# Dilated values loaded one unit sooner and the plain queries behind them, in a banded attention and top-1 expert kernel

## The chip, the core and the metric

The kernel runs on one core of a Trainium2 chip. The metric is the device time of one execution in microseconds (us), as the median of several runs. Five engines work beside each other: TensorE (PE, matrix products and transposes; PEld is its loading of weights), VectorE (DVE), ScalarE (ACT), GpSimd (POOL) and SyncE (SP), which here does little else than issue DMAs. Each engine works off its own instructions in order.

## The reference

Eight batches of eight heads attend over 576 positions of 64 values each. Heads 0 to 3 are plain: a query sees the 32 positions up to itself. Heads 4 to 7 are dilated: a query sees every fourth position back to 128. The attended rows (4608 tokens of 512 values) then go through a mixture of eight experts, of which each token takes the one with the highest gate.

```python
scores = scale * np.matmul(q, k.transpose(0, 1, 3, 2))
rel = pos[:, None] - pos[None, :]
mask_plain = (rel >= 0) & (rel < window)
mask_dil = (rel >= 0) & (rel < window * dilation) & (rel % dilation == 0)
masks = np.stack([mask_plain if h < H // 2 else mask_dil for h in range(H)], axis=0)
scores = np.where(masks[None, :, :, :], scores, -1000000000.0)
...
return np.matmul(attn, v).astype(np.float32)
```

```python
logits = x @ w_gate + modality_bias[modality_id]
e_idx = np.argmax(logits, axis=1)
...
    h = np.maximum(x[mask] @ w1[e], 0.0)
    out[mask] = gate_w[mask, None] * (h @ w2[e])
```

## The kernel before

The attention comes first and the experts after it. The attention is cut into 72 units, nine for each batch `b`, counted by `m` from 0 to 8 within the batch and by `t` over all. A unit takes two blocks of 64 queries with all four heads of a kind. Units 0 to 3 are plain (`kd == 0`), unit 4 takes the last block of each kind, and units 5 to 8 are dilated (`kd == 1`). For the dilated heads the positions are sorted by their rest modulo 4, so that the band is as narrow as that of the plain ones.

A loop over `t` writes the order of work out by hand: under the manual schedule PE, DVE, ACT and SP keep the order in which the loop emits instructions. One pass `t` emits the scores of unit `t` (line 340, and the adding of the mask on DVE at line 343), the exponential of unit `t-1`, the products with the values of unit `t-3` (`attend`, line 365), the gate logits of unit `t-5`, the transposes of the probabilities of unit `t-2`, the store of unit `t-4`, then the copies `shift_v` (ACT, line 137), and then the transposes of queries and keys that a coming unit needs (`qk_chunks`: PE at line 306, ACT copies at 309 and 311). `step()` and `advance()` put in work of the experts and of the routing.

The loads for a batch are sixteen DMAs of 144 KB for queries and keys of both kinds, and 1152 KB of values, half of it for each kind:

- `load_one` (line 116) loads queries or keys of one kind, in four DMAs, one for each head, into one of four buffers `st`. The transposes of `qk_chunks` read them. There are six pieces for a kind, keys and queries in turn; for the plain kind the first two pieces need heads 0 and 1 only, the next two heads 2 and 3, and the last two all four. Two pieces are done in a pass: the plain ones of batch `b+1` in passes `m` = 4, 5 and 6 of batch `b`, the dilated ones in passes 8, 0 and 1.
- `load_v` loads the values into one of three buffers `vw`: the plain ones in one DMA (line 127), the dilated ones in twelve small ones (line 131), because each block of 64 sorted positions may touch two residues. `shift_v` then copies the last 32 rows of each block to the top of the next, one head in pass 4, one in pass 5 and two in pass 6 for the dilated kind. One head's copy reads eight of the nine blocks, which the first eleven of the twelve DMAs fill.

The dilated values of batch `b+1` go to the buffer that held the plain values of batch `b`. Its last reader is `attend` of unit 4, which pass 7 emits.

All these loads are issued by SP in the order in which the loop emits them. For one batch before the change that is: keys of the plain kind in pass 6 (for two batches ahead), queries of the plain kind in pass 7, the first six pieces of the dilated values in pass 8, the other six at the start of pass 0, dilated keys in pass 1, dilated queries in pass 2 and plain values in pass 3.

After the eighth batch's units the experts run in slots of 256 tokens. The first slots are filled from the routing of the first five batches: POOL gathers their rows into `xr`, SP writes these to `x_slot` and reads them back as `xg` in passes of the last two batches.

Of the kernel before, what the change touches and what calls it, by code (L numbers as in the profile page):

```python
# [22 lines left out]
B, H, S, D = 8, 8, 576, 64  # L23
# [28 lines left out]
def _csegs(c0, c1):  # L52

    segs, c = [], c0
    while c < c1:
        r = c // CL
        n = min(c1, (r + 1) * CL) - c
        segs.append((c - c0, r, c - r * CL, n))
        c += n
    return segs  # L60
# [4 lines left out]
def kernel(  # L65
# [43 lines left out]
    def vw(b, kd):  # L109
        return vws[(2 * b + kd) % 3]  # L110

    def load_one(b, kd, src, queue=nc.sync):

        t = ald.tile([PQ, SI, 4, D], F32, name="st")
        for h in range(4):
            queue.dma_start(out=t[:, :, h], in_=src[b, 4 * kd + h].rearrange("(p s) d -> p s d", s=SI))
        return t

    def load_qk(b, kd, queue=nc.sync):
        kn = load_one(b, kd, k)  # L120
        return load_one(b, kd, q, queue), kn

    def load_v(b, kd, part=slice(None)):

        t = vw(b, kd)
        if kd == 0:
            nc.sync.dma_start(out=t[WIN:KW, :, :, 0:D], in_=v[b, 0:4].rearrange("h (i p) d -> p h i d", p=TQ))
        else:
            vv = v[b, 4:8].rearrange("h (j r) d -> r j h d", r=NCLS)
            for i, o, r, j, n in [(i, *seg) for i in range(NTILE) for seg in _csegs(TQ * i, TQ * (i + 1))][part]:  # L130
                nc.sync.dma_start(out=t[WIN + o:WIN + o + n, :, i, 0:D], in_=vv[r, j:j + n])
        return t

    def shift_v(b, kd, h):

        t = vw(b, kd)
        nc.scalar.copy(out=t[0:WIN, h, 1:NTILE].rearrange("p i d -> p (i d)"), in_=t[TQ:KW, h, 0:NTILE - 1].rearrange("p i d -> p (i d)"))

    state = {('qk', 0, 0): load_qk(0, 0, nc.scalar)}
# [142 lines left out]
    def qk_chunks(kd, qn, kn):  # L282


        def chunk(n, is_q):
            src = qn if is_q else kn
            pt = psum['o'].tile([P, 512], F32, name="po") if is_q and psum['many'] else ps_t.tile([P, 512], F32, name="pt")
            flat = qT[kd] if is_q else kT[kd][:, :, WIN:]
            inp = pt[:, 0:4 * PQ]
            if kd == 0:  # L290

                gs, s0, ns = ((n,), 0, 4) if n < 2 else ((0, 1), 4, 2)
                inp = inp.rearrange("c (g p i) -> c g p i", g=len(gs), i=ns)
                jobs = [(inp[:, x, :, i], s0 + i, g) for x, g in enumerate(gs) for i in range(ns)]
                parts = [(flat[:, gs[0]:gs[-1] + 1].rearrange("c g (p s) -> c g p s", s=SI)[:, :, :, s0:s0 + ns], inp)]
            else:
                inp = inp.rearrange("c (g i p) -> c g i p", g=2, p=PQ)
                jobs = [(inp[:, g, i], 2 * n + i, g) for g in range(2) for i in range(2)]

                parts = []  # L300
                for e in range(2):
                    o = 6 * e + 2 * n
                    dst = flat.rearrange("c g (r j t) -> c g r t j", r=NCLS, t=3)[:, :, o % 4:o % 4 + 2, o // 4]
                    parts.append((dst, inp.rearrange("c g i (j e) -> c g i e j", e=2)[:, :, :, e]))
            for to, i, g in jobs:
                nc.tensor.transpose(out=to, in_=src[:, i, 2 * g:2 * g + 2].rearrange("p a d -> p (a d)"), identity=ident[:PQ, :PQ])
            for dst, src in parts:
                if is_q:
                    nc.scalar.mul(dst, src, 1.0 / 8.0)
                else:  # L310
                    nc.scalar.copy(out=dst, in_=src)
        return [(lambda n=n, is_q=is_q: chunk(n, is_q)) for n in range(SI // 2) for is_q in (False, True)]
# [368 lines left out]
    NU = len(order)  # L681
# [233 lines left out]
    units, pieces, dilated = [], [], []  # L915
# [11 lines left out]
    def step(share=MOE_RATE / 6):  # L927

        nonlocal credit
        if moe:  # L930
            credit += share if state['t'] < NU else 1
            while credit >= 1:
                credit -= 1
                next(moe, None)

    def advance(some=range(-1, B)):
        for b, task in tasks:
            if b in some:
                next(task, None)

    state['routed'] = False
    for t in range(NU + LAG + 1):
        state['t'] = t
        if 'go' in state and not moe:
            octx.close()
            psum['many'] = False
            psum['y'] = ctx.enter_context(tc.tile_pool(name="ps_y", bufs=2, space=PSUM))
            psum['o'] = ctx.enter_context(tc.tile_pool(name="ps_o1", bufs=1, space=PSUM))
            moe = slots(NS, ids_of, ahead, hold)
        b, m = t // 9, t % 9  # L950
        if t == 1:
            pieces = qk_chunks(1, *state['qk', 0, 1])
        if t < NU:
            jobs = order[t][1]
            if m == 0:
                state['lT', b] = gwk.tile([2 * NE, S], F32, name="lT")
            if b + 1 < B:
                if m == 4:
                    pieces = qk_chunks(0, *state['qk', b + 1, 0])
                elif m == 8:  # L960
                    pieces = qk_chunks(1, *state['qk', b + 1, 1])
            if m == 0 and b > 0:
                load_v(b, 1, slice(6, None))
            elif m == 3:
                if b + 1 < B:
                    state['v', b + 1, 0] = load_v(b + 1, 0)
            units.append(Unit(b, m, jobs, [state['v', b, 0], state['v', b, 1]] if m >= 4 else [state['v', b, 0]], state['lT', b]))
            units[t].scores()
        step()
        if 0 <= t - 1 < NU:  # L970
            units[t - 1].exp()
        po = psum['o'].tile([P, 512], F32, name="po")
        if 0 <= t - 3 < NU:
            units[t - 3].attend(po)
        step()
        if 0 <= t - LAG < NU:
            units[t - LAG].logits(po)
        if 0 <= t - 3 < NU:
            units[t - 3].normalize()
        if 0 <= t - LAG < NU:  # L980
            units[t - LAG].gather_logits()
            if (t - LAG) % 9 == 8:
                tasks.append(((t - LAG) // 9, background((t - LAG) // 9)))
        step()
        advance()
        if 0 <= t - 2 < NU:
            units[t - 2].probsT()
        step()
        if 0 <= t - 4 < NU:
            units[t - 4].store()  # L990
            units[t - 4].keep(pool)

        for h in {0: (0,), 1: (1,), 2: (2, 3)}.get(m, ()) if 2 < t < NU else {0: (0, 1), 1: (2, 3)}.get(t, ()):
            shift_v(b, 0, h)
        for h in {4: (0,), 5: (1,), 6: (2, 3)}.get(m, ()) if t < NU else ():
            shift_v(b, 1, h)
        for i in range(2):
            step()
            if i < len(pieces):
                pieces[i]()  # L1000
        pieces = pieces[2:]
        if t < NU and b + 1 < B:

            if m == 1:
                state['k', 1] = load_one(b + 1, 1, k)
            elif m == 2:
                state['qk', b + 1, 1] = load_one(b + 1, 1, q), state['k', 1]
            elif m == 6 and b + 2 < B:
                state['k', 0] = load_one(b + 2, 0, k)
            elif m == 7 and b + 2 < B:  # L1010
                state['qk', b + 2, 0] = load_one(b + 2, 0, q), state['k', 0]
            elif m == 8:
                state['v', b + 1, 1] = load_v(b + 1, 1, slice(0, 6))
        advance([*round_of, B - 1] if moe and t < NU else range(-1, B))


# [40 lines left out]
```

## Time and profile before

| what | value |
|---|---|
| time, median of 3 runs | 711.53 us (710.65 to 712.71) |
| time of the profiled execution | 710.85 us |
| span of the profiled execution, first to last instruction | 709.1 us |
| busy share of the span: PE, DVE, ACT, POOL | 92%, 70%, 62%, 41% |
| mean granted TensorE clock | 0.959 of full speed |
| first score of the attention, last score of the attention | 14.59 us, 252.10 us |

Times in rows are microseconds from the start of the span. In a row of the timeline the first number is the start, the second the duration, then come engine, line, operation, what is written and read, and in square brackets the idle time of the engine just before the row with what ended it. "x12" says that the row merges twelve instructions that follow each other. A DMA row on SPq lasts as long as SP needs to issue; when the data lands is not in it, and shows only where somebody waits for it.

### The profile page before, as it was taken

The page shows a single profiled execution, that of the slowest core. Times are in us where ns is not written, and L with a number is a line of the kernel's source. Part 1 is how long each engine was busy: PE and PEld are TensorE (multiplying, and loading weights), DVE is VectorE, ACT ScalarE, POOL GpSimd, SP SyncE. Part 2 cuts the span into 40 slices and gives each one's busy share as a digit, 9 for nine tenths or more (in the row PEclk, how much of TensorE's full clock was granted, in tenths as well). Part 3 has the DMA queues.
Part 4 walks back from the last instruction along what each step waited for, and adds up shares of the span by engine and source line. Part 5 has one row for each costly group of instructions (what it writes and reads, how often), then busy time and mean ns, then how long its engine had stood idle before and what let it go on. Part 6 is the DMA issues. An engine that isn't in the chain of part 4 may idle for free. (4 is left out here: it accounts for less than half of the span.)

```text
span 709.1 us, 17888 instructions
## 1 busy us (share of the span) xinstructions
PE 649.3 (92%) x6286; PEld 571.1 (81%) x6286; DVE 497.4 (70%) x1212; ACT 437.9 (62%) x964; POOL 290.0 (41%) x396
## 2 busy tenths in 40 slices
PE   6799998997887899799999999999999999999991
PEld 3688787786776688689999999999999999999980
DVE  1688886886876778677766776667766677667660
ACT  3587896886766656355665565565666556655650
POOL 7345774865668553533333232233313231310110
PEclk7799999999899699999999999999999999999996
DMA  9898698697976943213433972333222346821730
GB/s 159 144 233 180 150 193 169 150 195 145 166 167 159 257 131 77 61 61 91 138 131 78 263 185 79 74 114 106 96 83 82 99 120 182 219 74 46 203 86 13
DMA packets 163233, 94.95 MB, mean 134 GB/s; under 512 B 124144, under 2 KB 143090, under 8 KB 163140
## 3 DMA queue, kind: packets, MB, share of 16 engines
q1 hardware_dynamic: 146612, 63.89, 40.3%
q0 software_dynamic: 11120, 28.64, 13.4%
q10 hardware_dynamic: 5408, 1.24, 1.0%
q8 instruction: 51, 0.84, 0.6%
q14 instruction: 42, 0.34, 0.2%
HBM read 127.52 MB, written 29.39 MB: 221 GB/s over the span
## 5 line engine op out<-in xcount | busy, mean ns | idle before, releaser
L858 PE MATMUL pt<-xh,w1l 128*128 128x256 f32 (+1 forms) x608 | 172.9, 284 | 7.7 <-DVE w1l L807 7.7
L858 PE MATMUL pt<-xl,w1h 128*128 128x256 f32 (+1 forms) x608 | 172.3, 283 | 0.0
L858 PE MATMUL pt<-xh,w1h 128*128 128x256 f32 (+1 forms) x608 | 172.2, 283 | 0.0
L864 ACT ACTIVATE hh<-pt 128x256 fp32r<-128x256 f32 (+1 forms) x152 | 57.6, 379 | 159.5 <-PE pt L858 159.4
L807 DVE TENSOR_TENSOR w2l<-w2q,w2h 128x512 fp32r<-128x512 f32 x152 | 104.9, 690 | 43.0 <-ACT w2h L806 34.7
L274 POOL DMA_INDIRECT xr<-x_dram,idt x74 | 82.5, 1115 | 120.4 <-DMA x_slot<-xr 72.2
L858 PEld LDWEIGHTS pt<-xh,w1l 128*128 128x128 f32 x608 | 116.7, 192 | 8.6 <-DVE w1l L807 8.5
L858 PEld LDWEIGHTS pt<-xh,w1h 128*128 128x128 f32 x608 | 116.5, 192 | 6.8 <-ACT w1h L806 0.2
L858 PEld LDWEIGHTS pt<-xl,w1h 128*128 128x128 f32 x608 | 116.6, 192 | 5.7
L838 PE MATMUL py<-w2h,hh 128*128 128x512 f32 x296 | 118.1, 399 | 0.0
L838 PE MATMUL py<-w2h,hl 128*128 128x512 f32 x296 | 117.1, 396 | 0.0
L838 PE MATMUL py<-w2l,hh 128*128 128x512 f32 x296 | 116.1, 392 | 0.0
L865 DVE SCALAR_TENSOR_TENSOR hl<-pt,hh 128x256 fp32r<-128x256 f32 (+1 forms) x152 | 63.3, 416 | 73.9 <-ACT hh L864 73.8
L274 POOL DMA_INDIRECT out_dram<-ys,idt x37 | 39.6, 1071 | 179.4 <-ACT ys L841 115.8
L807 DVE TENSOR_TENSOR w1l<-w1q,w1h 128x512 fp32r<-128x512 f32 x152 | 104.1, 685 | 2.7 <-ACT w1h L806 2.7
L806 ACT CAST w1h<-w1q 128x512 fp32r<-128x512 f32 x152 | 94.4, 622 | 3.3 <-DMA w1q<-in_moe_w_dram 3.3
L806 ACT CAST w2h<-w2q 128x512 fp32r<-128x512 f32 x152 | 93.1, 612 | 0.0
L274 POOL TENSOR_TENSOR sm<-sm,nmx 128x384 f32<-128x384 f32 x72 | 59.8, 830 | 61.9 <-DVE den L372 45.5
L365 PE MATMUL po<-vw,pT 96*64 96x65 f32 x1152 | 57.0, 238 | 11.3 <-ACT pT L359 6.7
L359 ACT COPY pT<-pt 96x512 f32<-96x512 f32 x72 | 41.5, 576 | 41.3 <-PE pt L356 40.2
L838 PEld LDWEIGHTS py<-w2l,hh 128*128 128x128 f32 x296 | 55.8, 189 | 13.2
L365 PEld LDWEIGHTS po<-vw,pT 96*64 96x64 f32 x1152 | 44.5, 145 | 24.6 <-ACT pT L359 11.4
(160 smaller groups left out, 1110.7 us busy)
## 6 DMA issues: line engine op xcount, KB each, us to landing
w2q<-in_moe_w_dram SPq DMA_DIRECT2D x76, 512.0 KB
w1q<-in_moe_w_dram SPq DMA_DIRECT2D x152, 256.0 KB
st<-in_k_dram SPq DMA_DIRECT2D x64, 144.0 KB
x_slot<-xr SPq DMA_DIRECT2D x18, 512.0 KB
xg<-x_slot SPq DMA_DIRECT2D x72, 128.0 KB
x_dram<-x_sb POOLq DMA_DIRECT2D x32, 256.0 KB, 3.6
st<-in_q_dram SPq DMA_DIRECT2D x56, 144.0 KB
vw<-in_v_dram SPq DMA_DIRECT2D x8, 576.0 KB
```

What stands on the lines that cost most here:

```text
L274: ins = tc.keep_in_program_order(getattr(nc.gpsimd, name)(*args, **kw))
L359: nc.scalar.copy(out=self.pT, in_=src)
L365: nc.tensor.matmul(out=pov[u * TQ:(u + 1) * TQ, h, :], lhsT=self.pT[:, h, u * TQ:(u + 1) * TQ], rhs=self.vts[kd][:, h, i, :], start=True, ...
L806: nc.scalar.copy(out=hi, in_=raw)
L807: nc.vector.tensor_tensor(out=lo, in0=raw, in1=hi.bitcast(F32), op=ALU.subtract)
L838: nc.tensor.matmul(out=py[u], lhsT=ht[:, us], rhs=wt, start=(f + n == 0), stop=(f + n == FC + 1))
L858: nc.tensor.matmul(out=ph, lhsT=wt[:, c, :], rhs=xt[:, c, 0:cols], start=(c + i == 0), stop=(c + i == KC + 1))
L864: nc.scalar.activation(out=hh, in_=ph, func=AF.Relu)
L865: nc.vector.scalar_tensor_tensor(out=hl, in0=ph, scalar=0.0, in1=hh.bitcast(F32), op0=ALU.max, op1=ALU.subtract)
```

## The change

The dilated values of the next batch are issued in passes 7 and 8 instead of 8 and 0 (the second half now at the end of pass 8 and not at the start of pass 0). The plain queries, which stood in pass 7, are issued at the end of pass 0 of the next batch, behind all twelve value pieces. In batch 0, the six pieces of dilated transposes, two in each of passes 1, 2 and 3, are done three at once in passes 2 and 3, and the copies `shift_v` of the plain values move from passes 0 and 1 to passes 1 and 2.

```diff
-        if t == 1:
+        if t == 2:
             pieces = qk_chunks(1, *state['qk', 0, 1])
...
-            if m == 0 and b > 0:
-                load_v(b, 1, slice(6, None))
-            elif m == 3:
+            if m == 3:
                 if b + 1 < B:
                     state['v', b + 1, 0] = load_v(b + 1, 0)
...
-        for h in {0: (0,), 1: (1,), 2: (2, 3)}.get(m, ()) if 2 < t < NU else {0: (0, 1), 1: (2, 3)}.get(t, ()):
+        for h in {0: (0,), 1: (1,), 2: (2, 3)}.get(m, ()) if 2 < t < NU else {1: (0, 1), 2: (2, 3)}.get(t, ()):
             shift_v(b, 0, h)
...
-        for i in range(2):
-            step()
+        at_once = 3 if t < 4 else 2
+        for i in range(at_once):
+            if i < 2:
+                step()
             if i < len(pieces):
                 pieces[i]()
-        pieces = pieces[2:]
+        pieces = pieces[at_once:]
...
-            elif m == 7 and b + 2 < B:
-                state['qk', b + 2, 0] = load_one(b + 2, 0, q), state['k', 0]
+            elif m == 7:
+                state['v', b + 1, 1] = load_v(b + 1, 1, slice(0, 6))
             elif m == 8:
-                state['v', b + 1, 1] = load_v(b + 1, 1, slice(0, 6))
+                load_v(b + 1, 1, slice(6, None))
+            elif m == 0 and b > 0:
+                state['qk', b + 1, 0] = load_one(b + 1, 0, q), state['k', 0]
```

## Rows read from the trace of the kernel before

**Rows 1.** Windows: PE, PEld, DVE, ACT, POOL busy, granted clock, DMA share.

```profile
45.00:75.00 30.00, 28.35 (x516) 24.40 (x513) 25.83 (x85) 25.23 (x63) 16.57 (x28) 1.00 0.82 182
300.00:650.00 350.00, 347.46 (x2209) 315.13 (x2210) 249.80 (x450) 208.50 (x430) 103.28 (x93) 1.00 0.41 117
```

**Rows 2.** Timeline of DVE, line 343: first unit of batches 1 to 6, last unit.

```profile
44.91 0.56 DVE L343 TENSOR_TENSOR sm<-pss,masks 128x384 f32<-128x384 f32 x1
...
71.67 0.54 DVE L343 TENSOR_TENSOR sm<-pss,masks 128x384 f32<-128x384 f32 x1
...
98.19 0.54 DVE L343 TENSOR_TENSOR sm<-pss,masks 128x384 f32<-128x384 f32 x1
...
128.14 0.54 DVE L343 TENSOR_TENSOR sm<-pss,masks 128x384 f32<-128x384 f32 x1
...
155.20 0.54 DVE L343 TENSOR_TENSOR sm<-pss,masks 128x384 f32<-128x384 f32 x1
...
187.87 0.54 DVE L343 TENSOR_TENSOR sm<-pss,masks 128x384 f32<-128x384 f32 x1
...
252.10 0.51 DVE L343 TENSOR_TENSOR sm<-pss,masks 128x384 f32<-128x384 f32 x1
```

**Rows 3.** Timeline of ACT, first copy of the dilated values in batches 3 and 5.

```profile
115.66 0.62 ACT L137 COPY vw<-vw 32x520 f32<-32x520 f32 x1 [3.91 <-DMA st<-in_k_dram]
...
173.60 0.62 ACT L137 COPY vw<-vw 32x520 f32<-32x520 f32 x1 [4.83 <-DMA st<-in_k_dram]
```

**Rows 4.** Waits up to 300 us: total, times, longest (these are batches 2, 4).

```profile
ACT vw L137 <- DMA vw<-in_v_dram: 2.4, 2, 1.5
```

**Rows 5.** Timeline of SP: loads around the dilated values of batches 1 to 7.

```profile
48.00 8.01 SPq L131 DMA_DIRECT2D vw<-in_v_dram  x12
...
70.58 2.68 SPq L116 DMA_DIRECT2D st<-in_q_dram  x4
73.36 9.58 SPq L131 DMA_DIRECT2D vw<-in_v_dram  x12
...
97.96 3.55 SPq L116 DMA_DIRECT2D st<-in_q_dram  x4
101.61 10.15 SPq L131 DMA_DIRECT2D vw<-in_v_dram  x12
...
125.42 2.98 SPq L116 DMA_DIRECT2D st<-in_q_dram  x4
128.50 9.19 SPq L131 DMA_DIRECT2D vw<-in_v_dram  x12
...
152.40 4.07 SPq L116 DMA_DIRECT2D st<-in_q_dram  x4
156.57 14.14 SPq L131 DMA_DIRECT2D vw<-in_v_dram  x12
...
183.31 2.91 SPq L116 DMA_DIRECT2D st<-in_q_dram  x4
...
206.24 0.78 SPq L127 DMA_DIRECT2D vw<-in_v_dram  x1
216.25 0.40 SPq L645 DMA_DIRECT2D x_slot<-xr  x1
```

**Rows 6.** Waits of SP over the span: total, times, longest.

```profile
SPq L131 <- DMA vw<-in_v_dram: 3.7, 3, 2.8
SPq L131 <- DMA st<-in_q_dram: 3.2, 5, 1.1
```

**Rows 7.** Timeline of PE, first transposes of plain queries in pass 4 of batch 3.

```profile
111.19 0.49 PE L306 MATMUL po<-ident,st 96*128 96x96 f32 x4
```

**Rows 8.** Timeline of PE, the same transposes in pass 4 of batch 0.

```profile
32.37 0.52 PE L306 MATMUL po<-ident,st 96*128 96x96 f32 x4 [1.38 <-DMA st<-in_q_dram]
```

**Rows 9.** Timeline of SP, the load that these transposes read.

```profile
27.52 2.60 SPq L116 DMA_DIRECT2D st<-in_q_dram  x4
```

**Rows 10.** Timeline of PE, products with the values in pass 7 of batch 5.

```profile
183.48 0.69 PE L365 MATMUL po<-vw,pT 96*64 96x65 f32 x16 [0.29 <-ACT pT L359]
```

## The prediction

> **What bounds the kernel now.** I looked first at the stages, by windows. From 300 us on, TensorE is busy 347.46 of 350 us, and in the attention 28.35 of 30 us when nothing stalls [rows 1]. The change touches loads of the attention only. The last unit of the attention starts at 252.10, and 709.1 - 252.10 = 457.0 us of experts and their routing follow [rows 2]. PE is full there, so I count what the attention gains or loses one to one at the end.
>
> Then I looked at how long a batch takes, from the first unit of one to that of the next [rows 2]: 26.8 us for batch 1 (71.67 - 44.91), 26.5 for batch 2, 29.95 for batch 3, 27.1 for batch 4, 32.7 for batch 5. Three batches agree within 0.6 us and two stick out. The waits say why. ACT's first copy of the dilated values, in pass 4, waited 3.91 us in batch 3 and 4.83 us in batch 5 [rows 3], and 2.4 us in batches 2 and 4 together, the longer one 1.5 us, so 0.9 and 1.5 us [rows 4]. The rows name keys as the releaser in the two long cases, but this copy reads no keys. The values' twelve DMAs are what it needs, and these had just been issued: SP ended them at 101.61 + 10.15 = 111.76 in batch 3, with the copy starting at 115.66, and at 156.57 + 14.14 = 170.71 in batch 5, with the copy at 173.60 [rows 3, 5].
>
> A wait does not cost its whole length. Against 26.65 us (the mean of batches 1 and 2) batch 3 lost 3.3 us for 3.91 us of waiting, batch 4 0.4 for 1.5, batch 2 nothing for 0.9. So ACT has 0.6 to 1.1 us in hand. Batch 5 lost 6.0 us; I put 4.83 - 0.6 = 4.2 us of it down to the wait, and leave 1.8 us, since the routing for the first slots runs there and nothing here says otherwise. The values' lateness costs 3.3 + 0.4 + 4.2 = 7.9 us in all. That is what the change can win.
>
> **Values sooner.** No instruction is added or removed in a batch after the first: SP issues the same DMAs in another order. The twelve value DMAs take the place of the four of the queries, so they start sooner by what the queries took: 73.36 - 70.58 = 2.8 us in batch 2, 3.65 in batch 3, 3.1 in batch 4, 4.2 in batch 5 [rows 5]. If they land sooner by as much, the waits shrink to 0, 0.26, 0 and 0.66 us. Batch 2 shows that waits of this length cost nothing. So this part gives up to 7.9 us.
>
> **Queries later.** This is the price. The queries now end where the values ended. Who needs them next is PE: the first transposes of queries in pass 4 need heads 0 and 1, so the second of the four DMAs. In batch 3 they run at 111.19, 13.0 us after the batch's first unit [rows 2, 7]; I use 13.0 us for every batch. How long after its issue does such a DMA land? In batch 0 PE waited for just this until 32.37. SP issued the four from 27.52 in 2.60 us, so the second from 28.17, and it took 4.2 us [rows 8, 9]. Heads 2 and 3 are needed a pass (3 us) later but are issued only 1.3 us later, so they land in time if heads 0 and 1 do.
>
> The bound from above takes SP's stretch of sixteen DMAs as long as before. The second query DMA then starts 1.95 us (three quarters of 2.60) before the old end of the values, and lands 4.2 us after that. Batch 3: 111.76 - 1.95 + 4.2 = 114.0 against 111.19, so PE waits 2.8 us. Batch 5: 170.71 + 2.25 = 172.96 against 155.20 + 13.0, so 4.8 us. Batch 2: 82.94 + 2.25 = 85.2 against 84.7, so 0.5. Batch 1 (58.26 against 57.9): 0.35. Batch 4 (139.9 against 141.1): none. Sum 8.45 us, with nothing in hand to swallow it, since PE is the fullest engine [rows 1].
>
> The bound from below takes 8.01 us for the twelve values, which is what they took in batch 1 [rows 5]. The second query DMA then starts 8.01 + 0.65 us after the old start of the queries and lands 4.2 us after that, so 12.9 us after it: 110.8 in batch 3 against 111.19, 165.3 in batch 5 against 168.2, 83.4 in batch 2 against 84.7. No wait at all.
>
> Which is nearer? The twelve took 10.15 us in batch 3 and 14.14 in batch 5, because SP itself waited between them for earlier DMAs to land: for queries 3.2 us in five waits and for values 3.7 us in three [rows 6]. The five behind queries go away when the queries come after; those behind values, and whatever was slow in batch 5, may come back behind the keys. Both kinds of wait weigh about the same, so I take the middle: 4.2 us of waits on PE. **Sum: 7.9 - 4.2 = 3.7 us won**, with bounds of +7.9 and -0.55.
>
> [...] The row of windows shows DMA engines at 0.82 of their time in a batch without a stall [rows 1], and SP's rows leave gaps of 0.1 us between these loads [rows 5]. [...]
>
> **SP's new wait.** The first six values may go only after PE's products of unit 4, in pass 7. In batch 5 those end at 183.48 + 0.69 = 184.17, and SP would be there at 183.31 [rows 5, 10]: SP stands for 0.9 us, with the next queries and dilated keys behind it. Both are needed some 10 us or more later, since batch 6 starts at 187.87 and its pass 4 comes 13 us after. I cost it at nothing; were that cover gone, it would be 0.9 us. In the other batches SP arrives later than that pass. In batch 6 the first six values move ahead of `x_slot`, for which SP stood idle from 207.0 to 216.25 [rows 5]. They may delay it by up to 4 us, half of 8.01, and the second six then stand behind it. The read back to `xg` follows all of these in either order, so I cost it at nothing too.
>
> **Batch 0.** Moving the dilated transposes from pass 1 to 2 lets unit 2's scores go sooner, and moving the copies of the plain values keeps ACT free. But PE waits for batch 1's queries until 32.37 anyway, and their load, issued at 27.52, has nothing moved ahead of it [rows 8, 9]. Work that gets there sooner waits longer. Bounds: a win of 1.38 us were that wait to end sooner, and a loss of about 0.9 us, a third piece's share of PE (0.49 us as in rows 7) in each of two passes. I take 0, because the DMA decides.
>
> **The number.** 710.85 - 3.7 = 707.15 us for the profiled execution. The median of the runs lies 0.7 us above it, so 707.8 us.
>
> **The rivals.** First, the wait only moves: PE waits for queries as long as ACT did for values. For it speaks the bound from above, and SP's solid rows; against it, that a part of SP's waits was for the queries ahead. Between a loss of 0.55 and a win of 2 us this gives 709.5 to 712, say 711.5. Chance 0.23.
>
> Second, it is slower: PE's waits exceed ACT's, because a query DMA behind twelve values lands later than 4.2 us after issue. If 5.2 us, each of batches 1, 2, 3 and 5 waits 1 us more than in the bound from above: 8.45 + 4 = 12.45, against 7.9 won, which gives 716 us. It decides once the landing takes 4.6 us and more with SP's stretch unshortened: 0.55 + 4 x 0.4 = 2.15 us, the 0.3% that a measurement of this kernel can tell from no change. For it speaks that the values of batch 3 needed about 4 us after the last issue [rows 3, 5]; against it, that the values are light and leave little queued before the queries. Chance 0.12.
>
> Third, the values' wait goes and none comes: 711.5 - 7.9 = 703.6 us. For it speaks the bound from below. Chance 0.15. The forecast, between 705 and 709.4 us, has 0.50. So faster has 0.65, no change 0.23, slower 0.12.
>
> The range of 702.8 to 712.5 us reaches over the third and the first; the forecast's own is 705 to 709.4.
>
> **What would show it.** After: ACT's copies at line 137 without waits of over 1 us in batches 2 to 5, SP's twelve values ahead of the four queries and taking less than 10 us in batch 3, waits of some 1 to 2.5 us at PE's line 306 on `in_q_dram` in pass 4 of batches 3 and 5, batch 0 as long as before, and 457 us from the last unit on. The prediction is wrong if the waits at line 306 reach those of line 137 before, if slow landings fall elsewhere than in batches 3 and 5, or if the experts' stage gives time back.

## The result: slower by 0.47%

The changed kernel took 716.24 us (median of 20 runs, 711.43 to 719.87) and the kernel before 711.95 us on the same chip. The measured ratio is 1.0047, with a 95% interval of 1.0029 to 1.0065 (it is not the quotient of the two medians, which is 1.0060). Two repeats gave 1.0034 [1.0005, 1.0063] and 1.0030 [1.0002, 1.0057] (e5, e13). The forecast of 707.8 us was wrong, and its range of 702.8 to 712.5 us did not hold the time. The profiled execution took 714.13 us with a span of 712.4 us.

First the windows of the changed kernel, one for each batch from its first unit to that of the next (batches 1 to 6), then the stage of the experts. The columns are the stretch and its length, busy time of PE, PEld, DVE, ACT and POOL, then granted clock, DMA share and GB/s.

```profile
43.18:71.03 27.85, 25.13 (x459) 21.49 (x455) 22.78 (x76) 22.68 (x57) 13.83 (x25) 1.00 0.78 185
71.03:97.44 26.41, 24.86 (x451) 21.22 (x445) 22.62 (x76) 22.29 (x56) 19.00 (x30) 1.00 0.83 171
97.44:128.10 30.66, 26.47 (x449) 22.57 (x445) 22.56 (x76) 22.46 (x56) 18.91 (x30) 0.94 0.72 156
128.10:162.90 34.80, 27.46 (x452) 23.46 (x447) 22.86 (x76) 22.57 (x56) 18.99 (x30) 0.90 0.78 153
162.90:190.77 27.87, 25.82 (x467) 21.84 (x461) 23.97 (x88) 22.93 (x57) 19.79 (x30) 1.00 0.76 171
190.77:224.00 33.23, 27.39 (x428) 22.96 (x426) 25.04 (x89) 21.43 (x52) 22.62 (x34) 0.90 0.65 160
...
300.00:650.00 350.00, 345.21 (x2189) 312.76 (x2190) 249.05 (x454) 206.33 (x424) 104.22 (x95) 0.99 0.41 117
```

Batches 2 and 5 lose nothing now, and batch 5 shows that it needs 27.9 us by itself, more than the others. Batches 3 and 4 stick out. Batch 1 starts 1.7 us sooner than before (43.18 against 44.91), batches 1 to 5 take 147.6 us against 143.0, and batch 6 starts 2.9 us later [rows 2]. Batch 6 takes 33.2 us against 31.7, and batch 7 gives 2.6 us back, so that the last unit stands 1.84 us later (253.94 against 252.10):

```profile
253.94 0.52 DVE L343 TENSOR_TENSOR sm<-pss,masks 128x384 f32<-128x384 f32 x1
```

From there 458.5 us follow, against 457.0 before. The waits say what happened. ACT's copies at line 137 wait for no load any more [rows 3, 4]. PE does instead, in the timeline of its transposes of the plain queries (batches 0, 1, 3 and 4):

```profile
30.97 0.52 PE L306 MATMUL po<-ident,st 96*128 96x96 f32 x4 [1.91 <-DMA st<-in_q_dram]
...
57.73 0.52 PE L306 MATMUL po<-ident,st 96*128 96x96 f32 x4 [1.09 <-DMA st<-in_q_dram]
...
113.27 0.55 PE L306 MATMUL po<-ident,st 96*128 96x96 f32 x4 [2.65 <-DMA st<-in_q_dram]
...
147.16 0.87 PE L306 MATMUL po<-ident,st 96*128 96x96 f32 x4 [5.82 <-DMA st<-in_q_dram]
```

SP's timeline gives the issue of what they read (values, then queries, in batches 1, 3 and 4; in the last two of these the row of queries is cut after the second DMA):

```profile
43.29 8.87 SPq L131 DMA_DIRECT2D vw<-in_v_dram  x12
52.20 2.63 SPq L116 DMA_DIRECT2D st<-in_q_dram  x4
...
96.34 8.82 SPq L131 DMA_DIRECT2D vw<-in_v_dram  x12
...
106.93 1.25 SPq L116 DMA_DIRECT2D st<-in_q_dram  x2
...
127.19 11.11 SPq L131 DMA_DIRECT2D vw<-in_v_dram  x12
...
138.34 1.28 SPq L116 DMA_DIRECT2D st<-in_q_dram  x2
```

The second DMA starts at 52.20 + 2.63/4 = 52.86 and its data is used at 57.73, 4.9 us later. In batch 3 that is 113.27 - (106.93 + 0.63) = 5.7 us, in batch 4 147.16 - (138.34 + 0.64) = 8.2 us. In batches 2 and 5 it landed before PE needed it. The prediction took 4.2 us for each. This wait also cost more than its length. Windows of 2 us around the wait in batch 4:

```profile
139.00:141.00 2.00, 1.98 (x40) 1.70 (x33) 1.61 (x5) 1.03 (x4) 1.34 (x2) 1.00 0.23 53
141.00:143.00 2.00, 0.33 (x4) 0.15 (x2) 1.18 (x5) 1.73 (x4) 0.82 (x1) 1.00 0.59 172
143.00:145.00 2.00, 0.00 (x0) 0.00 (x0) 0.00 (x0) 0.00 (x0) 0.00 (x0) 1.00 1.24 261
145.00:147.00 2.00, 0.00 (x0) 0.00 (x0) 0.00 (x0) 0.00 (x0) 0.00 (x0) 0.76 1.25 77
147.00:149.00 2.00, 1.84 (x22) 1.61 (x26) 0.31 (x2) 0.91 (x2) 0.00 (x0) 0.50 0.83 172
149.00:151.00 2.00, 2.00 (x33) 1.66 (x28) 1.44 (x4) 0.11 (x1) 0.10 (x1) 0.50 1.21 209
151.00:153.00 2.00, 2.00 (x13) 1.97 (x12) 1.17 (x6) 0.96 (x3) 1.40 (x4) 0.53 0.91 142
153.00:155.00 2.00, 2.00 (x44) 1.70 (x43) 1.33 (x3) 1.95 (x5) 0.57 (x1) 1.00 1.07 234
```

While PE waits, PE, DVE, ACT and POOL all come to a stop (0.00 busy from 143 to 147 us). The granted clock falls to 0.50 late in the wait: by windows of half a microsecond it is 1.00 up to 146.0 us, 0.56 from 146.0 to 146.5 and 0.50 from there to 152.5, so it stays there for over 5 us after the wait, with PE busy all the time. In that stretch the scores of a unit (line 340) took 0.92 us of PE (148.55 us), and behind it 0.56 us (153.26 us).

### The profile page after: what moved, and what is told of

It reads as the page before. It is cut to its first block, busy times and chain, and to the rows that moved or that the text cites. A ratio compares the mean times of both kernels' runs of the same rounds, so it can differ in the third digit from the quotient of the medians.

```text
span 712.4 us, 17870 instructions
## 1 busy us (share of the span) xinstructions
PE 648.6 (91%) x6286; PEld 570.6 (80%) x6286; DVE 497.1 (70%) x1212; ACT 438.2 (62%) x964; POOL 289.3 (41%) x396
## 4 chain that ended last, share of the span: by engine, by line
PE 53%; issue 2%; DVE 1%; DMA 1%; ACT 0%; POOL 0%; POOLq 0%; ACTq 0%
PE pt L858 27%; PE py L838 26%; DMA out_dram<-ys,idt 1%; POOL out_dram L274 0%; DVE w1l L807 0%; ACT w2h L806 0%; ACT ys L841 0%; ACT w1h L806 0%; POOLq L1025 0%; DVE ge L569 0%; DVE ge L563 0%; DVE bs L571 0%; DVE cn L532 0%; DVE es L565 0%; DVE bs L594 0%
```

## The experiments

The theory after the result: the queries of heads 0 and 1 now arrive too late, and that is the loss. The rivals: the edits of batch 0 cost it; the first six values, behind unit 4's products, hold up SP; or the loss is chance. A second question is where the 7.9 us went that the sooner values should have won. Ratios are to the kernel before on the same chip, with 95% intervals; on the chips of the experiments its median was 706.2 to 707.7 us, so times are compared on one chip only.

**Which part loses.** e1 is the kernel before with the edits of batch 0 alone, e2 the new order of loads alone, e5 and e13 the whole change again. e1, on the kernel before (e2 is the rest of the change's diff):

```diff
-        if t == 1:
+        if t == 2:
...
-        for h in {0: (0,), 1: (1,), 2: (2, 3)}.get(m, ()) if 2 < t < NU else {0: (0, 1), 1: (2, 3)}.get(t, ()):
+        for h in {0: (0,), 1: (1,), 2: (2, 3)}.get(m, ()) if 2 < t < NU else {1: (0, 1), 2: (2, 3)}.get(t, ()):
...
+        at_once = 3 if t < 4 else 2
...
-        pieces = pieces[2:]
+        pieces = pieces[at_once:]
```

> The kernel before with batch 0's part of the change alone (dilated transposes three at once in passes 2 and 3, the copies of the plain values a pass later); every load stays where it was. If the loss of the change comes from the queries behind the values, this part is harmless: batch 1's first unit, which the changed kernel started 1.7 us sooner (43.2 us against 44.9), starts as much sooner here too, and the time is 1 to 2 us below the kernel before. If batch 0's part is what loses, this kernel is about 3 us slower than the kernel before.

> The changed kernel with batch 0 as before: only the order of the loads is changed. If the queries behind the values lose the time, this is slower than the kernel before by what the changed kernel loses (about 4 us) and the 1 to 2 us that batch 0 gives it, so by 4 to 6 us, with waits on the queries at PE's line 306 of 5 to 12 us in all. If batch 0's part loses, it is level with the kernel before or faster.

> The changed kernel itself, beside the kernel before on the chip of the three runs that follow, and for a second profile of it. Both theories expect a ratio of 1.003 to 1.0065, as measured before. Which batches wait for queries may change from one execution to the next; if the waits belong to the program they stand in batches 1, 3 and 4 again (1.1, 2.7 and 5.8 us), and if slow landings come at random they stand elsewhere.

> The changed kernel as it is. If PE's wait for the queries of heads 0 and 1 is what it loses, the ratio is again 1.003 to 1.005 and above that of the split kernel beside it by 0.003 or more. If the loss of 0.47% was chance, the ratio comes within 0.3% of 1 and no more than 0.001 above the split kernel's.

e1: 0.9983 [0.9959, 1.0007]. e2: 1.0034 [1.0005, 1.0062]. e5: 1.0034 and e13: 1.0030, as above. The order of the loads carries the loss; batch 0 does not, and the 1 to 2 us expected of e1 aren't told from nothing. In e2 the longest wait of PE falls in batch 4 again, and in e5 in batch 5, so the batch that is hit changes from one execution to the next. Spans of the changed kernel were 712.4, 701.8 (e5) and 707.6 us (e13). That holds for the kernel before as well. In e1, whose loads are in the old order, ACT's waits for loads in batches 1 to 5 are shorter than those of [rows 3, 4], and fall in batches 2 to 4:

```profile
ACT vw L137 <- DMA st<-in_k_dram: 3.5, 1, 3.5
...
ACT vw L137 <- DMA vw<-in_v_dram: 2.4, 2, 2.0
```

So a profile is one execution out of a spread: that of e5 was the shortest of its twelve runs, that of e1 the longest.

**Was there a win to have?** e4 keeps the old order and removes ACT's wait from the other side: the first copy of the dilated values goes one pass later.

```diff
-        for h in {4: (0,), 5: (1,), 6: (2, 3)}.get(m, ()) if t < NU else ():
+        for h in {5: (0, 1), 6: (2, 3)}.get(m, ()) if t < NU else ():
             shift_v(b, 1, h)
```

> The kernel before, with ACT's copies of the dilated values in passes 5 and 6 (two heads each) and not in passes 4, 5 and 6. No load moves; the values are needed some 3 us later. If ACT's waits for them (11.2 us in the profile of before) cost what the lengths of the batches say (7.9 us), the time falls by 4 to 8 us. If they were slack that another wait takes over, the time stays within 2 us of the kernel before.

Measured: 0.9999 [0.9970, 1.0028]. No copy and no transpose waits for a load in batches 1 to 5, and batch 6 starts at 181.24, 6.6 us sooner than before [rows 2]. But then POOL gets to its first gather of rows for the experts and waits for the ids (numbers of the rows to gather), with the softmax of batch 6 queued behind it. Timeline of POOL, first for the kernel before and then for e4:

```profile
204.83 1.09 POOL L274 DMA_INDIRECT xr<-x_dram,idt  x1 [3.81 <-DMA idt<-table]
```

```profile
202.06 1.09 POOL L274 DMA_INDIRECT xr<-x_dram,idt  x1 [7.63 <-DMA idt<-table]
```

Batch 6 by windows takes 35.57 us at a clock of 0.86, where it took 31.69 before (the kernel before first):

```profile
187.87:219.56 31.69, 27.15 (x442) 22.74 (x437) 25.36 (x89) 22.12 (x53) 22.33 (x33) 0.95 0.64 153
```

```profile
181.24:216.81 35.57, 28.28 (x441) 24.27 (x437) 25.25 (x89) 22.14 (x53) 22.34 (x33) 0.86 0.63 148
```

The last unit starts at 248.97, 3.1 us sooner, and the span is 708.2 against 709.1. Beside the one profile of the kernel before, over half of the gain is gone in batch 6, most of the rest in the experts, and over the runs nothing is left.

**What lateness costs.** e9 is the changed kernel with the queries one more pass later, e10 the kernel before with its second six values moved from the start of pass 0 to the end of pass 1. In both the moved loads stand behind the four dilated key loads. e9, on the changed kernel (e10 puts the second `load_v` of the kernel before in the same place):

```diff
             if m == 1:
                 state['k', 1] = load_one(b + 1, 1, k)
+                if b > 0:
+                    state['qk', b + 1, 0] = load_one(b + 1, 0, q), state['k', 0]
...
-            elif m == 0 and b > 0:
-                state['qk', b + 1, 0] = load_one(b + 1, 0, q), state['k', 0]
```

> The changed kernel with the plain queries put off once more, behind the four dilated key loads (both at the end of pass 1). That makes the second query DMA some 2.6 to 3 us later. If PE pays for late plain queries in full, the time rises by 5 to 13 us above the changed kernel (2.6 us in two to five batches), with waits at PE's line 306 on the queries in most of batches 1 to 5. If the loss of the changed kernel is not in these waits, it rises by 2 us at the most.

> The mirror of it on the kernel before: the second six value DMAs are put off behind the four dilated key loads in pass 1, 2.6 to 3 us later. If ACT's waits on values cost as much as PE's on queries, the time rises as much as with the queries put off (5 to 13 us). If ACT has slack, as the copies put a pass later suggest, it rises by half of that or less.

e9: 1.0175 [1.0132, 1.0218]. e10: 1.0142 [1.0089, 1.0194]. In e9 all of batches 1 to 5 wait, by PE's timeline:

```profile
61.16 0.87 PE L306 MATMUL po<-ident,st 96*128 96x96 f32 x4 [3.17 <-DMA st<-in_q_dram]
...
91.22 0.52 PE L306 MATMUL po<-ident,st 96*128 96x96 f32 x4 [0.62 <-DMA st<-in_q_dram]
...
120.36 0.52 PE L306 MATMUL po<-ident,st 96*128 96x96 f32 x4 [2.72 <-DMA st<-in_q_dram]
...
150.16 0.52 PE L306 MATMUL po<-ident,st 96*128 96x96 f32 x4 [1.46 <-DMA st<-in_q_dram]
...
178.49 0.52 PE L306 MATMUL po<-ident,st 96*128 96x96 f32 x4 [1.93 <-DMA st<-in_q_dram]
```

Undisturbed, a batch takes 26.75 us (batch 1) and 26.4 (2 to 4), as in e15, and 27.9 (5), as in the changed kernel and e13. In e9 the five take 32.8, 27.1, 30.7, 28.2 and 31.4 us. So waits of 3.17, 0.62, 2.72, 1.46 and 1.93 us cost 6.1, 0.7, 4.3, 1.8 and 3.5 us. In the changed kernel 1.09, 2.65 and 5.82 us cost 1.1, 4.3 and 8.4 us. ACT's copies in e10 waited as follows, and batches 3, 4 and 5 there took 27.95, 30.4 and 31.3 us, so that 1.02, 4.12 and 3.30 us cost 1.6, 4.0 and 3.4 us:

```profile
116.70 0.63 ACT L137 COPY vw<-vw 32x520 f32<-32x520 f32 x1 [1.02 <-DMA vw<-in_v_dram]
...
146.39 0.62 ACT L137 COPY vw<-vw 32x520 f32<-32x520 f32 x1 [4.12 <-DMA vw<-in_v_dram]
...
175.93 0.62 ACT L137 COPY vw<-vw 32x520 f32<-32x520 f32 x1 [3.30 <-DMA vw<-in_v_dram]
```

Over all such waits above 0.6 us, those of PE (12 waits in the changed kernel, e2, e5, e9 and e13) sum to 29.5 us and the excess of their batches to 48.3 us, 1.64 for one. Those of ACT (12 waits in the kernel before, e1, e7 and e10) sum to 32.0 us and cost 31.9 us, 1.0 for one. These are means of what such batches lost. Single ones scatter (PE's from 1.0 to 2.9 for one, ACT's from 0.1 to 1.5), and a batch can lose time without any wait for a load: batches 2 to 4 of e14 had none of 0.3 us or more on PE, DVE, ACT or POOL, yet took 27.5 to 27.6 us, with one unit in each whose scores took 0.92 us of PE (82.73, 110.51 and 138.29 us), where e15 with the same order took 26.4 and had no such row. Window of batch 2 of e14:

```profile
71.84:99.44 27.60, 26.08 (x451) 22.31 (x446) 22.83 (x76) 22.32 (x56) 19.03 (x30) 0.94 0.83 175
```

Just before those 0.92 us PE was busy 0.40, 0.61 and 0.85 us in the three microseconds from 79 to 82 us. At the same place e15 has 0.41, 0.61 and 0.85 us (79.5 to 82.5 us), and there the scores took 0.56 us (82.91 us). So what slowed PE isn't shown, and part of the 1.64 may not belong to the waits.

**Getting the queries there in time.** e3 does the three pieces of keys ahead of the three of queries, so that queries are needed later. e6 and e14 issue the queries of heads 0 and 1 in the old place and only those of heads 2 and 3 behind the values; e15 is that without batch 0's edits. e11 and e12 let GpSimd issue the plain queries, e11 in the changed kernel and e12 in the kernel before. e3, on the changed kernel:

```diff
                     pieces = qk_chunks(0, *state['qk', b + 1, 0])
+                    pieces = pieces[0::2] + pieces[1::2]
```

e6 and e14, on the changed kernel (`heads` and `t` are new arguments of `load_one`: which heads to load, and into which buffer):

```diff
             elif m == 7:
+                if b + 2 < B:
+                    state['qk', b + 2, 0] = load_one(b + 2, 0, q, heads=range(2)), state['k', 0]
                 state['v', b + 1, 1] = load_v(b + 1, 1, slice(0, 6))
...
             elif m == 0 and b > 0:
-                state['qk', b + 1, 0] = load_one(b + 1, 0, q), state['k', 0]
+                load_one(b + 1, 0, q, heads=range(2, 4), t=state['qk', b + 1, 0][0])
```

e11, on the changed kernel (e12 adds `pool` to the call that stands in pass 7 of the kernel before):

```diff
             elif m == 7:
+                if b + 2 < B:
+                    state['qk', b + 2, 0] = load_one(b + 2, 0, q, pool), state['k', 0]
...
-            elif m == 0 and b > 0:
-                state['qk', b + 1, 0] = load_one(b + 1, 0, q), state['k', 0]
```

> The changed kernel, with the six pieces of plain transposes done in another order: the three of keys first, then the three of queries. Still two in a pass, so the first queries are needed in pass 5 and not in pass 4, some 3 us later, and no load moves. If PE's waits on late queries are the loss (9.6 us in batches 1, 3 and 4 of the changed kernel's profile), most of them go, and the time is 6 to 9 us below the changed kernel, so 2 to 5 us below the kernel before. If the loss lies elsewhere (in the last two batches, behind the rows for the first slots, or in batch 0), this is level with the changed kernel, 3 to 4 us above the kernel before.

> The changed kernel with the plain queries in two halves: heads 0 and 1, which PE needs in pass 4, stay in pass 7 ahead of the values; heads 2 and 3, needed in pass 5, come behind the values at the end of pass 0. If PE's waits on heads 0 and 1 are the loss, the time falls 4 to 6 us below the changed kernel, to the kernel before or 1 to 2 us below it. If the loads as a whole are late and the waits only move to the next reader, it gains 2 us at the most against the changed kernel.

> The changed kernel with the queries of heads 0 and 1 ahead of the second six values. If those two heads are what the changed kernel loses, the ratio is 0.997 to 1.001 and TensorE's waits for queries at the first transposes stay below 1.5 us in batches 1 to 5. If something else in the change costs the time, such as the wait of the first six values or the work of batch 0, the ratio stays at 1.003 or above, as without the split.

> The split order without the change's edits of batch 0. If those edits are worth nothing, as predicted, the ratio agrees with that of the split kernel with them to 0.002. If they win the 1.38 us that the prediction gave as their bound, the ratio is 0.002 higher than with them.

> The changed kernel with the plain queries issued by POOL in pass 7 and not by SP: the values stay sooner, the queries are not behind them, and SP issues four DMAs less in a batch (2.6 us). POOL pays about 0.7 us for each of the four, as for its stores of x. If the late queries are the loss and SP's queue makes them late, the time falls 4 to 8 us below the changed kernel and below the kernel before as well. If the DMA engines and not SP's queue make the loads late, or POOL's 2.9 us a batch stall the softmax, it is level with the changed kernel or slower.

> The kernel before with the same: plain queries issued by POOL in pass 7, everything else as it was. SP then reaches the values four DMAs sooner, as in the changed kernel. If SP's queue is what makes the values late and that costs time, it is 2 to 6 us faster than before. If neither, it is level; if POOL's 2.9 us a batch matter, it is slower.

e3: 1.0025 [0.9998, 1.0053], with seven shorter waits of PE (5.3 us, the longest 1.4) and waits of ACT at line 137 again (2.7 us): inconclusive. e6: 0.9999 [0.9970, 1.0028], e14: 0.9999 [0.9971, 1.0026], e15: 1.0001 [0.9977, 1.0026], against 1.0034 and 1.0030 for the unsplit ones beside e6 and e14. None of these intervals is apart from the unsplit kernel's. Compared directly with the split runs on the same chip, though, the unsplit kernel is slower each time, by the means of the runs: e5 1.9 us above e6 (95% interval 0.0 to 3.7), e13 2.4 above e14 (0.4 to 4.3) and 2.9 above e15 (0.8 to 5.0). And PE's waits for queries in batches 1 to 5 fell to 0.4, 0 and 0.8 us (in e6 ACT's copies waited 3.9 us). The rest of the order is still in e15, SP's wait for unit 4 included, so that is not the loss. e15 beside e14 shows that the edits of batch 0 are worth nothing measurable.

e11: 1.0096 [1.0060, 1.0131]. e12: 1.0121 [1.0075, 1.0167]. Nothing waits for a load in batches 1 to 5 of either, yet both lose, in e11 by this group of POOL between 40 and 200 us (count, busy us, mean ns):

```profile
L274 POOL DMA_DIRECT2D st<-in_q_dram x24 | 17.6, 740 | 0.0
```

Four of these take 3 us out of POOL in one pass, and the softmax on POOL stands behind them, as in batch 2 of e11:

```profile
94.71 0.83 POOL L274 TENSOR_TENSOR sm<-sm,nmx 128x384 f32<-128x384 f32 x1 [0.47 <-ACT pe L351]
...
96.51 2.94 POOL L274 DMA_DIRECT2D st<-in_q_dram  x4
...
100.79 0.84 POOL L274 TENSOR_TENSOR sm<-sm,nmx 128x384 f32<-128x384 f32 x1
```

SP spends nearly as long on four (2.63 us at 52.20 above), but it has no softmax behind them.

**Where the gain of the sooner values went.** e7 is the kernel before with one edit: in batch 6 the dilated keys and queries of batch 7 are issued one pass later, so that SP's read of the ids isn't behind them. e8 has the edits of e1, e4 and e7, e16 those of e14 and e7. e7, on the kernel before:

```diff
-            if m == 1:
+            late = b == EARLY[0][0] + 2
+            if m == 1 + late:
                 state['k', 1] = load_one(b + 1, 1, k)
-            elif m == 2:
+            elif m == 2 + late:
```

> The kernel before with batch 6's dilated keys and queries loaded a pass later, so that SP gets to the ids of the first slots ahead of the four dilated key loads. If what the attention gains is taken back where POOL waits for these ids (3.8 us in the profile of before, 7.6 us in the run with the copies a pass later), that wait falls by 2.5 to 3 us and the time by 1 to 3 us. If that wait is slack, the time is level with before within 1 us.

> The kernel before with three edits at once: batch 0's part of the change, the copies of the dilated values in passes 5 and 6, and batch 6's dilated loads a pass later (so the ids go ahead). No load of values or plain queries moves. If the copies a pass later won nothing only because POOL's wait for the ids took it back, this wins 4 to 8 us on the kernel before. If the experts' start takes it back in any case, it wins 2 us at the most.

> The split order, with batch 6's dilated keys and queries asked for one unit later, so that the ids of the first expert slots come sooner. If a gain of the sooner values is hidden by GpSimd's wait for these ids, the wait falls from some 3 to 6 us to 2 or less and the ratio to 0.996 or below. If the sooner values gain nothing once the queries are in time, the ratio stays within 0.2% of that of the split kernel.

e7: 0.9998 [0.9969, 1.0028]. e8: 0.9986 [0.9959, 1.0014]. e16: 0.9957 [0.9933, 0.9981], 703.81 us where the kernel before took 706.77: the one version here that is faster than both kernels. Timeline of POOL and window of batch 6, first for e14 and then for e16:

```profile
201.19 1.10 POOL L275 DMA_INDIRECT xr<-x_dram,idt  x1 [5.55 <-DMA idt<-table]
```

```profile
182.51:215.93 33.42, 27.99 (x441) 23.91 (x437) 25.26 (x89) 22.11 (x53) 22.32 (x33) 0.90 0.69 163
```

```profile
197.85 1.09 POOL L275 DMA_INDIRECT xr<-x_dram,idt  x1 [3.70 <-DMA idt<-table]
```

```profile
182.22:212.57 30.35, 25.77 (x442) 21.45 (x437) 25.06 (x88) 22.02 (x53) 22.35 (x33) 1.00 0.77 173
```

The wait fell by 1.9 us, to 3.70 where 2 or less was expected, but the clock stayed up (1.00 against 0.90) and batch 6 became 3.1 us shorter, about the 3.4 us between the medians of e14 and e16 (707.18 and 703.81; by the means e16 is 3.1 us faster, 1.2 to 5.0). Neither the loads in time alone (e14, e15) nor the ids sooner alone (e7) moves the time clear of noise; the two together do in e16.

e8 says that this is not the whole account. It too has no wait for a load in batches 1 to 5 and the ids sooner (their wait is 1.28 us), and yet isn't told from the kernel before. One thing that sets it apart from e16 is that its values stand in the old order. Batch 7 by windows, first for e8 and then for e16:

```profile
212.90:245.87 32.97, 25.05 (x367) 20.43 (x365) 22.72 (x73) 19.86 (x46) 21.48 (x32) 0.80 0.89 220
```

```profile
212.57:242.62 30.05, 24.21 (x372) 20.05 (x372) 23.09 (x74) 19.65 (x45) 21.45 (x32) 0.83 0.87 213
```

Batch 7 takes 29.3 to 30.0 us in the four profiles of the changed order (the changed kernel, e2, e5, e13) and 31.8 to 34.2 us in those of the old one (the kernel before, e1, e4, e7, e8). So with the sooner values batch 7 is some 2 us or more shorter. In e7 and e8 a later gather of POOL waits 2.33 and 1.97 us in batch 7, which it does not in e16; whether that is the reason wasn't tested. (With the queries issued by GpSimd, batch 7 took 32.3 us in e11 and 30.6 in e12, so the order of the values isn't all.)

Nor is it shown that whoever gets past the loads sooner always stands longer at the ids. In the old order it is so: batch 6 starts at 187.87, 184.63 and 181.24 us in the kernel before, e1 and e4, and the waits are 3.81, 7.30 and 7.63 us. But e5 starts it at 183.28 and waits 3.33 us, and the changed kernel at 190.77 and waits 6.20 us.

## Why the prediction was wrong

- **What bounds; one to one at the end.** From the last unit to the end of the span it took 457.0 us before, 458.5 after, and 457 to 460 us in the experiments' profiles. So the time at the last unit counts about one to one, within 4 us. What fails is to count a gain of batches 1 to 5 so: batch 6 stands between, and in e4 it gave back over half.
- **"The values' lateness costs 7.9 us in all. That is what the change can win."** This step failed: the first sentence held, the second did not. The waits are real (ACT's vanished, and e10 shows what more of them costs). By the undisturbed lengths they cost the batches 9.0 us in that one execution, 7.2 us in e1 and 6.7 in e7, in other batches. But taking them away did not win this: e4 had none of them and was level with the kernel before (0.9999), e14 and e15, which had none either, were level too, and e16 won 3.0 us (706.77 - 703.81) with the ids sooner as well. In e4 the time was lost again in batch 6, where POOL waits for the ids; that this holds for the other versions is argued, not shown.
- **Batch 5.** The 1.8 us that were left unexplained are mostly batch 5's own length, 27.9 against 26.65 us.
- **Values sooner.** Right: no copy waited, and the twelve values of batch 3 took 8.82 us, under 10. What the sum left out is batch 7, which came out some 2 us or more shorter with the sooner values.
- **"Queries later", 4.2 us.** The second failing term, in two ways. The landing of 4.2 us came from one load in batch 0 and was 4.9, 5.7 and 8.2 us here. PE waited 9.6 us in batches 1, 3 and 4, above the upper bound of 8.45 us. In other executions it was less (e5 3.0, e13 2.6, e2 5.3 us; 5.1 us as the mean of the four), so the 4.2 us were low but not far off as a mean. But they were counted one to one, and batches with such waits lost 1.64 for one: for 4.2 us this makes 6.9 us. With that alone the sum would still be a small win, 7.9 - 6.9 = 1.0 us; the loss needs the failure above as well, that the 7.9 us do not come back. The loss of 0.3 to 0.47% is 2.1 to 3.3 us; how much of PE's loss is hidden at the ids in turn isn't settled.
- **The first rival, that the wait only moves.** Of the waits themselves this is what came: 9.6 us of PE for 11.1 us of ACT. It gave the time of before because it counted both alike. The time was not that of before, though: the same DMAs in another order cost 0.34% in e2 and 1.75% in e9. SP's rows were nearly solid (gaps of 0.1 us between most of these loads) and its order still decided who got the data in time.
- **SP's new wait and batch 0.** Costed at nothing, rightly as far as the runs tell: e15, which has SP's wait for unit 4, is level with the kernel before, and so is e1, which has the edits of batch 0. In the changed kernel batch 0 took 29.3 us (43.18 - 13.92) against 30.3 us (44.91 - 14.59), though PE waited longer in it, 1.91 us against 1.38 [rows 8].
- **The rivals.** The second came true, by the sign that it had named: the landing took over 4.6 us, and the change lost. Its price of 716 us rested on 7.9 us won and waits at one to one, two errors against each other, so the agreement with 716.24 us is no proof of its sum. The prediction also named what would make it wrong, slow landings outside batches 3 and 5; batch 4 was one. Which batch was hit changed from one execution to the next, so to name it right would have been luck.

## What to carry to other kernels

Take the size of a wait for DMAs from several executions before counting it as a gain, and ask which wait comes next in the chain: here a start of batch 6 some 6 us sooner left nothing in the time of the runs, and batch 6 stood longer at a gather that waited for its ids (7.63 us against 3.81). When two loads compete for one queue, order them by what stands still if each is late; a late operand of the fullest engine cost more than its wait here (1.64 us for one, as a mean). Split a load where its parts are needed at different times before moving it whole.

## What the runs showed of the hardware

- TensorE's clock. In a wait of 5.82 us without a matmul (batch 4 of the changed kernel) the granted clock fell to 0.50 some 5 us after the last matmul, stood there for over 5 us of unbroken work behind the wait, and was at 1.00 from 153 to 157 us; the whole cost 8.4 us. In batch 6 of e4, with a wait of 7.63 us at the ids, it was 0.86 on average, and 0.95 in the kernel before with a wait of 3.81 us. It was also below 1.00 where no load was waited for (0.94 on average in batch 2 of e14, whose batches 2 to 4 were 1.1 to 1.2 us longer than in e15). What makes it fall and rise is not shown beyond these rows.
- The same load behind the same DMAs landed 4.9, 5.7 and 8.2 us after its issue in one execution, in the three batches where PE waited for it, and the batch with the longest wait changed from one execution to the next.
- A DMA of 144 KB issued by GpSimd took 740 ns of that engine (mean of 24 in e11). Four of them in a pass, ahead of the softmax, went with a loss of 0.96% (e11) and 1.21% (e12), though no load was waited for in batches 1 to 5.
